# Turning tiles with the DMA engines instead of TensorE, on SyncE's queue, in a new instruction order

## The chip, the cores and the metric

The kernel runs on one core of one Trainium2 chip. The metric is the time on the device in microseconds (us). An execution has a state, fast or slow, given with each run: slow here means over 1.5% above the fastest run of the same kernel. Ratios below use fast runs alone, while the medians quoted are of all runs.

The engines: TensorE (PE for matmuls, PEld for loading weights), VectorE (DVE), ScalarE (ACT), GpSimd (POOL), SyncE (SP, which here does nothing but issue DMAs; "SPq" is its issue queue). Sixteen DMA engines move the data that all of them ask for.

## The reference

A gated delta rule over 4 batches of 8 heads, 768 tokens and 48 channels, followed by a mixing layer over tokens and channels:

```python
k_n = k / (np.linalg.norm(k, axis=-1, keepdims=True) + 1e-06)
for t in range(S):
    readout = np.einsum('bhd,bhde->bhe', q[:, :, t], state)
    y[:, :, t] = g[:, :, t] * readout
    v_old = np.einsum('bhde,bhd->bhe', state, kt)
    state = state + bt[:, :, :, None] * np.einsum('bhd,bhe->bhde', kt, vt - v_old)
# x: y with its heads side by side, (4, 768, 384)
theta = x @ w_theta
zr, zi = x * cos(theta), x * sin(theta)
u = x + einsum('ts,bsd->btd', w_tok_r, zr) + einsum('ts,bsd->btd', w_tok_i, zi)
return u + np.maximum(u @ w_ch, 0.0)
```

## The kernel before

The recurrence is worked in chunks of 128 tokens. There are 24 chunk tiles (4 batches of 6). For each, the kernel loads k, v and g, scales k, turns it (tokens to columns), forms two products of keys and queries, solves a triangular system, reads the state out, gates with g to get x, turns x, multiplies it by `w_theta`, takes sine and cosine, mixes over tokens with turned token weights, turns the mixed rows u and multiplies them by `w_ch`. Four kinds of tile are thus turned: keys (`kt`, 4 blocks of 128x128 each), x (`xT`, 3 blocks), mixed rows (`uT`, 3) and token weights (`wtokT`, 12 tiles of 6).

Every step is an operation with a name, its engine or a choice of engines ("ways"), and the pools that it takes a buffer from. A list `ORDER` holds the sequence of all 1,300 or so operations with the way of each; the instructions of each engine are issued in that order and each engine works through its own in order. So the place of an operation in `ORDER` is a schedule.

```python
SIZES = dict(
    k_raw=11, v_raw=6, g_raw=5, ktil=6, q_buf=2, qt=3, wtok=2, ksq=2, vs=5, kt=4, mt=4, at=4,
    x0=3, xa=3, xb=3, xT=3, sc=4, ut=3, uT=3, o=3, bank=8,
)
...
    def load(name, b, c):                      # k, v, g: all from SyncE
        def emit(way):
            src = {"k": k, "v": v, "g": g}[name]
            t = live[f"{name}{b}.{c}"] = sb(f"{name}_raw", [128, H, D], FP32)
            nc.sync.dma_start(t, src[b, :, c * C:(c + 1) * C, :].rearrange("h t d -> t h d"))
        add(f"{name}{b}.{c}", "SP", emit, (), ((f"{name}_raw", 0),))
...
        def emit_kt(way):                      # turn on TensorE, into PSUM
            t = live[f"ktp{n}"] = ps16(f"kt{n}")
            for p in range(NP):
                nc.tensor.transpose(
                    t[:, p, :], live[f"ktil{n}"][:, 2 * p:2 * p + 2, :].rearrange("p a d -> p (a d)"), ident
                )

        def emit_ke(way):                      # copy out of PSUM, on ACT or DVE
            live[f"kt{n}"] = sb("kt", [128, NP, C], BF16)
            evac(way)(live[f"kt{n}"], live.pop(f"ktp{n}")[:, 0:NP, :])
            done_with(f"kt{n}")
...
        def emit_out(way, x=""):               # stores: from SyncE too
            at0 = cols * halves.index(x)
            nc.sync.dma_start(out[b, tl * 128:(tl + 1) * 128, at0:at0 + cols], live[f"o{n}"][:, at0:at0 + cols])
```

x and u are turned in the same way (`xt` and `xe`, `utt` and `ue`), and the token weights too (`wt` and `we`).

Of the kernel before, what the change touches and what calls it, by code (L numbers as in the profile page):

```python
# [10 lines left out]
FP32 = mybir.dt.float32  # L11
# [4 lines left out]
ACT = mybir.ActivationFunctionType  # L16
# [9 lines left out]
TABLE_BATCHES = 3  # L26

# [5 lines left out]
    49, 2116, 3335, 0, 1, 4, 23, 24, 10, 52, 2, 3, 25, 26, 69, 70, 71, 7428, 22, 205, 29, 207, 72, 208, 209, 2259, 7,  # L33
    73, 1292, 2492, 446, 2075, 28, 5, 30, 31, 13, 411, 1277, 32, 273, 447, 413, 8, 448, 414, 415, 2465, 2286, 47, 43,
    41, 213, 44, 206, 2260, 419, 240, 67, 45, 46, 214, 450, 452, 219, 220, 50, 42, 2289, 2269, 451, 2270, 239, 2096,
    242, 2271, 244, 2272, 210, 225, 1275, 2294, 215, 33, 19, 245, 37, 275, 226, 2466, 216, 34, 243, 38, 276, 420, 412,
    425, 227, 228, 277, 2327, 426, 278, 2331, 16, 2083, 36, 217, 39, 40, 2300, 2301, 218, 2475, 2295, 2302, 2303, 248,
    61, 2328, 2329, 90, 2476, 2304, 2305, 88, 308, 2298, 2477, 58, 76, 2306, 2307, 2139, 249, 2126, 84, 79, 260, 86,
    11, 2391, 274, 2137, 185, 2478, 261, 85, 200, 77, 310, 2359, 2330, 87, 4358, 285, 229, 4359, 2479, 2480, 416, 312,
    2362, 287, 2469, 6, 230, 288, 2299, 345, 2481, 53, 2394, 264, 445, 2482, 347, 2397, 316, 289, 290, 453, 55, 2122,  # L40
    2506, 2507, 2399, 2339, 2340, 2341, 64, 2128, 14, 309, 81, 2470, 75, 82, 83, 2342, 460, 313, 2363, 2471, 461, 449,
    2502, 2510, 318, 2511, 456, 2343, 479, 481, 2344, 464, 457, 2368, 465, 186, 514, 2530, 516, 56, 480, 187, 2345,
    2346, 2514, 2515, 483, 2472, 485, 486, 2565, 487, 2332, 435, 484, 2537, 104, 2167, 4564, 518, 4565, 1274, 110,
    488, 322, 188, 231, 491, 2568, 549, 9, 378, 92, 265, 522, 98, 2541, 2542, 323, 2398, 232, 2543, 2544, 203, 2252,
    115, 317, 2569, 2372, 2237, 2373, 2538, 120, 2503, 380, 2429, 190, 2545, 2546, 266, 286, 299, 267, 2369, 2159,
    116, 326, 327, 95, 348, 1272, 2401, 2403, 2547, 2548, 12, 300, 470, 328, 329, 519, 524, 113, 301, 302, 330, 382,
    2432, 2549, 319, 2550, 2434, 2404, 331, 114, 173, 2380, 2381, 125, 492, 126, 201, 526, 17, 101, 344, 357, 1291,
    2400, 129, 2250, 131, 130, 358, 112, 2551, 2402, 359, 360, 132, 2552, 2165, 118, 127, 128, 551, 107, 2409, 2435,
    2169, 122, 193, 2242, 2410, 2411, 552, 123, 59, 124, 233, 191, 54, 334, 2240, 515, 2412, 365, 2576, 303, 1295,
    471, 234, 523, 2577, 366, 617, 619, 51, 436, 235, 4463, 2668, 4464, 685, 530, 531, 687, 2736, 437, 304, 472, 473,  # L50
    93, 1273, 621, 2486, 623, 305, 15, 335, 650, 180, 2580, 2581, 439, 440, 625, 626, 553, 618, 383, 624, 622, 2603,
    441, 2582, 369, 20, 527, 62, 2583, 627, 2427, 629, 268, 2436, 630, 307, 557, 2679, 269, 2680, 652, 653, 2440,
    2681, 2433, 536, 18, 2441, 336, 370, 390, 2682, 371, 175, 2604, 537, 372, 525, 60, 394, 337, 395, 237, 270, 505,
    689, 57, 691, 690, 2743, 692, 2745, 538, 539, 635, 338, 636, 2741, 396, 397, 540, 236, 339, 340, 183, 148, 558,
    373, 2232, 306, 272, 550, 398, 399, 506, 178, 637, 638, 474, 541, 563, 400, 401, 3117, 374, 2437, 176, 179, 271,
    391, 375, 2768, 507, 21, 162, 177, 342, 2556, 139, 376, 628, 1070, 564, 402, 509, 403, 341, 565, 475, 476, 1278,
    566, 2687, 2688, 404, 654, 510, 2615, 2453, 656, 722, 2616, 2742, 96, 651, 664, 181, 99, 1029, 658, 657, 659, 377,
    1071, 2559, 723, 665, 666, 2561, 182, 724, 163, 2774, 667, 569, 2632, 133, 2200, 406, 1030, 570, 668, 669, 136,
    154, 142, 155, 407, 408, 655, 2708, 151, 2560, 2619, 2620, 670, 671, 641, 586, 1031, 2635, 672, 158, 443, 1039,
    174, 477, 2710, 2776, 554, 94, 642, 159, 409, 588, 410, 1040, 673, 674, 156, 1032, 2638, 195, 153, 145, 2607, 160,  # L60
    1041, 686, 157, 643, 2744, 1072, 2640, 644, 675, 66, 97, 161, 3121, 542, 699, 543, 645, 2609, 169, 2709, 646,
    2608, 171, 755, 167, 170, 165, 1042, 1033, 647, 700, 166, 701, 172, 2711, 676, 1079, 164, 1034, 1080, 478, 702,
    1035, 1043, 2746, 573, 677, 574, 168, 1081, 648, 196, 197, 757, 703, 704, 678, 679, 1036, 1037, 1074, 823, 109,
    102, 721, 825, 826, 705, 706, 1075, 134, 824, 2806, 1082, 1083, 828, 2881, 2883, 589, 827, 1076, 2610, 856, 2642,
    2644, 1049, 829, 831, 137, 1077, 707, 858, 198, 708, 830, 2247, 1050, 140, 832, 837, 649, 709, 859, 1288, 63, 860,
    2910, 861, 711, 2775, 710, 100, 1051, 838, 712, 839, 840, 1293, 2882, 2914, 2916, 575, 576, 734, 65, 442, 1052,
    103, 841, 735, 842, 1084, 1085, 996, 105, 725, 2778, 585, 2911, 146, 2639, 598, 577, 843, 544, 2641, 599, 600,
    844, 2780, 2626, 2777, 736, 1285, 601, 1059, 1044, 2912, 135, 857, 737, 845, 1045, 602, 603, 2645, 1086, 579,
    1280, 738, 545, 891, 604, 546, 1087, 998, 680, 580, 1053, 2884, 1060, 847, 581, 739, 846, 870, 2643, 2913, 893,
    740, 605, 583, 606, 848, 999, 1054, 849, 871, 1061, 894, 1055, 741, 895, 607, 892, 897, 548, 742, 743, 1088, 1062,  # L70
    1056, 2947, 582, 1057, 713, 714, 850, 681, 547, 2730, 872, 873, 1063, 608, 1089, 609, 874, 896, 759, 1090, 901,
    875, 2809, 2811, 2951, 610, 744, 745, 611, 2948, 756, 1091, 876, 1000, 1139, 3050, 877, 143, 769, 2781, 2810, 108,
    2812, 612, 770, 878, 1004, 1078, 613, 790, 792, 879, 793, 2779, 771, 614, 1140, 772, 715, 2732, 716, 746, 747,
    927, 926, 615, 851, 852, 4950, 1058, 880, 881, 1290, 1046, 1047, 1294, 616, 1141, 905, 717, 2917, 906, 1048, 773,
    774, 1142, 4949, 1143, 760, 2813, 1001, 3054, 898, 2815, 907, 908, 962, 1064, 1008, 1092, 1093, 775, 909, 1099,
    1119, 1282, 1065, 2915, 3055, 882, 2816, 928, 1094, 1066, 776, 1120, 910, 911, 777, 929, 138, 1100, 1067, 883,
    778, 930, 2980, 149, 1038, 795, 3143, 912, 1281, 2982, 1009, 1101, 719, 913, 106, 1005, 2848, 914, 779, 780, 144,
    1121, 2814, 781, 2850, 791, 782, 915, 997, 916, 931, 2984, 794, 2844, 902, 1122, 1123, 1109, 940, 941, 1096, 2846,
    2731, 804, 2983, 783, 1097, 3051, 2851, 961, 748, 749, 2849, 963, 964, 938, 2847, 1102, 1124, 1103, 141, 1129,
    2981, 942, 750, 1125, 751, 2832, 805, 2845, 1126, 943, 806, 807, 785, 944, 752, 1130, 754, 1127, 1128, 786, 1279,  # L80
    1110, 945, 808, 809, 1104, 3153, 1144, 1098, 946, 947, 1111, 810, 811, 1112, 1113, 1145, 1146, 1147, 812, 1148,
    939, 813, 1131, 1169, 4883, 948, 949, 2952, 814, 815, 2985, 753, 4884, 966, 3019, 3021, 965, 967, 917, 968, 918,
    1189, 1132, 950, 951, 952, 718, 3020, 953, 969, 1199, 1190, 1170, 954, 955, 816, 1114, 1200, 1106, 1133, 817,
    3163, 884, 885, 1283, 4885, 818, 975, 819, 821, 1171, 976, 1107, 820, 1108, 886, 3022, 970, 977, 978, 147, 1149,
    1134, 1135, 1201, 979, 980, 822, 919, 1136, 1137, 1068, 1172, 1173, 981, 1150, 982, 1202, 1203, 1191, 1159, 983,
    984, 1204, 3253, 1179, 1151, 985, 986, 1206, 1192, 1207, 1010, 1011, 1152, 1153, 1116, 1208, 987, 887, 889, 1117,
    1012, 1118, 1180, 1013, 888, 956, 957, 958, 960, 1160, 1138, 4951, 890, 1181, 1174, 1182, 1014, 3223, 1176, 988,
    1161, 2968, 921, 1162, 959, 1193, 1194, 1177, 1015, 1183, 922, 2972, 989, 990, 2971, 1289, 3243, 1016, 1184, 1209,
    1252, 1017, 2973, 1196, 1197, 1018, 1154, 1155, 991, 992, 3041, 3042, 1210, 1019, 1020, 1253, 1185, 1156, 150,
# [49 lines left out]
def kernel(  # L139
# [76 lines left out]
    def setup():  # L216
# [14 lines left out]
        for t in q_bufs:  # L231
            nc.vector.memset(t[:, H * NCH * D:], 0.0)

    BANK = (("bank", 0),)
    EVAC = ("ACT", "DVE")

    def evac(way):
        return (nc.scalar.copy, nc.vector.tensor_copy)[way]

    def mul_on(way):  # L240
        return (nc.gpsimd, nc.vector)[way].tensor_mul
# [549 lines left out]
```

## Time and profile before

| | before |
|---|---|
| time, median of 4 runs | 185.31 us (183.7 to 186.19) |
| profiled run: span, granted clock | 186.1 us, 0.978 (slow, barely) |
| transposes of the four kinds on TensorE | 312 (128 columns each) |
| instructions on SyncE's queue | 98 DMAs, no transpose |
| SyncE's queue: issuing / not issuing | 108 / 78 us |

An issue occupies the queue for some time before the next can start; in the view by source line, the loads of k read (columns: count, then least/median/greatest ns of one issue, then first and last start):

```profile
L255 SPq DMA_DIRECT2D k_raw<-in_k_dram x24: 418/882/4580, 0.8 to 74.1; - x24
```

So a plain load takes at least 0.4 us of that queue, 0.9 in the median and up to 4.6 (that one at 28.5 us, while the DMA engines are full). The mean of all 72 loads is 1.3 us; in the probe e5 below, which moves less at a time, the median is 0.59. The last k tile is asked for at 74.1 us. From the waits of SyncE's queue (columns here and in all tables of waits: us in total, times, longest us):

```profile
SPq L720 <- DVE o L712: 62.3, 14, 9.2
```

### The profile page before, as it was taken

How to read it: one execution, taken by the hardware profiler on the slowest of the kernel's cores; microseconds unless marked ns; L12 is line 12 of the kernel's file. 1: busy time of each engine (PE TensorE's matmuls, PEld its weight loads, DVE VectorE, ACT ScalarE, POOL GpSimd, SP SyncE). 2: the span in 40 equal slices, each digit the busy share in tenths (PEclk: the TensorE clock that was granted, in tenths of full speed). 3: DMA queues.
4: the chain of work that ended last, by engine and by line, in shares of the span. 5: the costliest groups of instructions: out<-in, count | busy, mean ns of one | idle time of the engine just before them, and what ended most of it. 6: DMA issues, size and time to landing. Idle time of an engine off the chain costs nothing.

```text
span 186.1 us, 6390 instructions
## 1 busy us (share of the span) xinstructions
PE 169.4 (91%) x2578; PEld 121.6 (65%) x2579; DVE 150.6 (81%) x330; ACT 116.5 (63%) x240; POOL 125.5 (67%) x173
## 2 busy tenths in 40 slices
PE   2878889659899999999999999999999999999992
PEld 0256577456777777777777777676777766666651
DVE  5685999718799999999999998988898678871472
ACT  2665789914889998899895858756632520443130
POOL 3469378199896999999999899989581330713000
PEclk9999999956999999999999999999999999999998
DMA  5999979999997999999982061094021132503043
GB/s 116 186 202 179 181 142 173 169 200 149 207 223 153 199 213 178 205 156 205 221 168 46 26 153 46 0 211 95 0 88 42 31 101 83 132 0 127 4 168 129
DMA packets 85150, 24.70 MB, mean 133 GB/s; under 512 B 75488, under 2 KB 85088, under 8 KB 85120
## 3 DMA queue, kind: packets, MB, share of 16 engines
q1 hardware_dynamic: 78528, 18.98, 47.9%
q0 software_dynamic: 6592, 5.31, 19.2%
q8 instruction: 20, 0.33, 0.7%
q14 instruction: 10, 0.08, 0.1%
HBM read 24.87 MB, written 4.72 MB: 159 GB/s over the span
## 4 chain that ended last, share of the span: by engine, by line
PE 71%; DMA 10%; DVE 7%; POOL 4%; ACT 3%; issue 2%; SPq 1%; DVEq 0%; POOLq 0%
PE bank L667 23%; PE bank L515 8%; PE bank L704 6%; PE bank L615 5%; PE bank L431 5%; DMA k_raw<-in_k_dram 5%; DMA wtok<-in_moe_w_tok_i_dram 4%; PE bank L409 3%; PE bank L376 3%; PE bank L286 2%; PE bank L689 2%; PE bank L577 2%; PE bank L247 2%; PE bank L604 2%; PE bank L574 2%
## 5 line engine op out<-in xcount | busy, mean ns | idle before, releaser
L667 PE MATMUL bank<-z_all,wtokT 128*128 128x384 bf16 x288 | 58.1, 326 | 0.0
L515 PEld LDWEIGHTS <-mt 128*128 128x128 bf16 x768 | 30.8, 97 | 11.3 <-issue 4.6
L667 PEld LDWEIGHTS <-wtokT 128*128 128x128 bf16 x288 | 24.8, 97 | 12.2
L483 DVE TENSOR_TENSOR xa<-x,bank 128x384 bf16<-128x384 bf16 x45 | 24.5, 549 | 6.2 <-issue 3.7
L629 POOL TENSOR_TENSOR z_all<-x_sb,sc 128x384 bf16<-128x384 bf16 x22 | 20.2, 927 | 11.3 <-ACT sc L619 11.2
L515 PE MATMUL bank<-xa,mt 128*128 128x48 bf16 x576 | 25.5, 184 | 2.0 <-ACT xa L481 1.1
L636 POOL TENSOR_TENSOR z_all<-x_sb,sc 128x384 bf16<-128x384 bf16 x18 | 16.7, 930 | 10.9 <-ACT sc L623 10.4
L457 POOL TENSOR_SCALAR_AFFINE_SELECT at<-at 128x512 bf16<-128x512 bf16 x33 | 20.6, 634 | 4.1 <-ACT at L449 4.1
L404 POOL TENSOR_TENSOR vs<-v_raw,sqrtb 128x384 bf16<-128x384 f32 x23 | 19.0, 829 | 5.0 <-DMA v_raw<-in_v_dram 4.9
L449 ACT ACTIVATE at<-bank 128x512 bf16<-128x512 f32 x33 | 18.5, 602 | 6.2 <-PE bank L431 5.7
L400 POOL TENSOR_TENSOR ktil_ring<-k_raw,kscale 128x384 bf16<-128x384 f32 x19 | 16.4, 866 | 7.8 <-DVE kscale L357 6.5
L619 ACT ACTIVATE sc<-bank 128x384 bf16<-128x384 f32 x24 | 11.9, 497 | 13.9 <-DVE z_all L634 7.8
L449 ACT ACTIVATE mt<-bank 128x512 bf16<-128x512 f32 x27 | 15.9, 600 | 5.6 <-PE bank L431 4.8
L693 ACT COPY uT<-bank 128x384 bf16<-128x384 bf16 x17 | 8.3, 486 | 14.8 <-PE bank L689 7.6
L457 POOL TENSOR_SCALAR_AFFINE_SELECT mt<-mt 128x512 bf16<-128x512 bf16 x27 | 16.7, 633 | 0.1
L683 DVE TENSOR_TENSOR ut<-x_sb,bank 128x384 bf16<-128x384 bf16 x23 | 12.5, 549 | 4.9 <-PE bank L667 4.5
L712 DVE SCALAR_TENSOR_TENSOR o<-bank,ut 128x384 f32<-128x384 f32 (+1 forms) x25 | 13.2, 538 | 3.8 <-PE bank L704 2.1
L431 PEld LDWEIGHTS <-kt 48*128 48x128 bf16 x384 | 11.6, 97 | 6.5 <-ACT kt L415 2.5
L704 PE MATMUL bank<-w_ch_sb,uT 128*128 128x384 bf16 (+1 forms) x75 | 15.5, 320 | 0.2
L615 PE MATMUL bank<-w_theta_sb,xT 128*128 128x384 bf16 x72 | 15.6, 325 | 0.0
L451 DVE TENSOR_TENSOR mt<-bank,neg_mask 128x512 bf16<-128x512 f32 x21 | 13.9, 681 | 0.7 <-PE bank L431 0.7
L583 DVE TENSOR_TENSOR x_sb<-bank,g_raw 128x384 bf16<-128x384 f32 x24 | 13.2, 549 | 0.8 <-PE bank L577 0.7
(102 smaller groups left out, 380.6 us busy)
## 6 DMA issues: line engine op xcount, KB each, us to landing
k_raw<-in_k_dram SPq DMA_DIRECT2D x24, 192.0 KB, 4.1
v_raw<-in_v_dram SPq DMA_DIRECT2D x24, 192.0 KB, 6.7
g_raw<-in_g_dram SPq DMA_DIRECT2D x24, 192.0 KB, 4.4
out_dram<-o SPq DMA_DIRECT2D x23, 192.0 KB, 2.0
q_buf<-in_q_dram POOLq DMA_DIRECT2D x4, 576.0 KB, 7.8
wtok<-in_moe_w_tok_r_dram POOLq DMA_DIRECT2D x3, 384.0 KB, 6.9
wtok<-in_moe_w_tok_i_dram POOLq DMA_DIRECT2D x3, 384.0 KB, 7.3
w_theta_sb<-in_moe_w_theta_dram POOLq DMA_DIRECT2D x1, 288.0 KB, 5.8
```

Source lines behind the costliest of these rows:

```text
L400: mul_on(way)(ktil[:, :, 0:D], live.pop(f"k{n}"), _bcast_last(kscale[:, b, c], D))
L404: mul_on(way)(t.rearrange("p (h d) -> p h d", d=D), live.pop(f"v{n}"), _bcast_last(sqrtb[:, b, c], D))
L431: nc.tensor.matmul(t[j][:, p, :], kt[r, p, :], moving[r, p, :], start=True, stop=True)
L449: nc.scalar.mul(dst, gram_ps, -1.0)
L457: nc.gpsimd.affine_select(out=t, in_=t, compare_op=ALU.is_gt, fill=0.0, base=0, pattern=[[0, NP], [1, C]], channel_multiplier=-1,)
L483: nc.vector.tensor_add(t, live[x_name], p_x)
L515: nc.tensor.matmul(p_x[:, h * D:(h + 1) * D], head(live[f"mt{n}"], h), live[cur][:, h * D:(h + 1) * D], start=not way, stop=not way or h = ...
L615: nc.tensor.matmul(p_th, xT[:, cb, :], w_theta_sb[:, cb, :], start=(cb == 0), stop=(cb == NB - 1))
L629: (nc.vector if way == 3 else nc.gpsimd).tensor_mul(z_all[:, b % 3, c, 0], xt, live[f"si{n}"][:, 0])
L636: nc.gpsimd.tensor_mul(z[:, 1], xt, sc[:, 1])
L667: nc.tensor.matmul(p_mix, wtokT[:, i, s, tl * 128:(tl + 1) * 128], z_all[:, b % 3, s, 1 - i, :], start=(i, s) == parts[0] and not way, sto ...
L704: nc.tensor.matmul(p_ffn, uT[:, cb, :], w_ch_sb[:, cb, at0:at0 + cols], start=(cb == 0), stop=(cb == NB - 1))
```

## The change

The intent: TensorE is the busiest engine, so take transposes off it. A DMA from SBUF to SBUF that transposes on the way needs neither TensorE nor PSUM nor a copy out of PSUM. Each of the four kinds of tile gets a third way, chosen per tile in `ORDER`; all DMA transposes are on SyncE's queue. `ORDER` is new altogether: 69 tiles (22 of keys, 24 of x, 19 of mixed rows, 4 of token weights; 241 blocks) go by DMA.

```diff
-    EVAC = ("ACT", "DVE")
+    EVAC, BY_DMA = ("ACT", "DVE"), 2
+    TURN, TURNED = ("PE", "PE", ""), EVAC + ("SP",)
...
         def emit_kt(way):
+            if way == BY_DMA:
+                return
             t = live[f"ktp{n}"] = ps16(f"kt{n}")
...
         def emit_ke(way):
             live[f"kt{n}"] = sb("kt", [128, NP, C], BF16)
+            if way == BY_DMA:
+                nc.sync.dma_start_transpose(live[f"kt{n}"], live[f"ktil{n}"].rearrange("p h d -> p (h d)"))
+                return
             evac(way)(live[f"kt{n}"], live.pop(f"ktp{n}")[:, 0:NP, :])
...
-        add(f"ke{n}", EVAC, emit_ke, (f"kt{n}",), (("kt", 0),), ((f"kt{n}", "bank"),))
+        add(f"ke{n}", TURNED, emit_ke, (f"kt{n}",), (("kt", 0),), turned(f"kt{n}"), with_=f"kt{n}")
```

(cut: the same for x, u and token weights; the bias of the cosine given as a constant instead of a tile; the new list.)

## The prediction

> **What bounds the kernel now.** I read the page's busy line first, then the slices, then a table of stretches, then single groups and the DMA part.
>
> ```profile
> PE 169.4 (91%) x2578; PEld 121.6 (65%) x2579; DVE 150.6 (81%) x330; ACT 116.5 (63%) x240; POOL 125.5 (67%) x173
> PE   2878889659899999999999999999999999999992
> PEclk9999999956999999999999999999999999999998
> DMA  5999979999997999999982061094021132503043
> ```
>
> TensorE is busiest. Its slices split the run in two: up to slice 12 (some 60 us) it has holes, afterwards it is full to the end. The DMA engines are the mirror image: full to about 100 us, mostly idle later. The granted clock falls to 5 and 6 tenths in two slices, at 37 to 46 us. The table of stretches (PE, PEld, DVE, ACT, POOL busy; then clock, DMA share, GB/s) says the same in numbers:
>
> ```profile
> 30.00:40.00 10.00, 6.00 (x124) 4.48 (x119) 5.94 (x14) 6.89 (x16) 5.52 (x8) 0.89 0.99 181
> 40.00:50.00 10.00, 9.22 (x153) 7.37 (x150) 7.07 (x15) 6.04 (x13) 9.37 (x15) 0.77 1.10 174
> 60.00:80.00 20.00, 19.24 (x364) 15.05 (x364) 19.68 (x41) 18.80 (x43) 19.45 (x25) 1.00 1.04 197
> 120.00:140.00 20.00, 20.00 (x319) 14.49 (x316) 17.39 (x39) 10.08 (x21) 15.48 (x23) 1.00 0.39 92
> 160.00:180.00 20.00, 20.00 (x168) 12.98 (x167) 11.70 (x25) 6.43 (x14) 5.18 (x6) 1.00 0.20 71
> ```
>
> Busy PE can hide slack, since matmuls overlap. So I took the spacing of starts instead of the durations: in the timeline around 121 us three 128-column transposes start at 121.38 and the next group at 121.55, so 57 ns each; three 384-column matmuls follow each other in 0.49 us in the chain, so 163 ns each; 16 of the 48-column ones in 0.40 us, so 25 ns each. Multiplying the instruction counts of each stretch by such spacings gives, of TensorE time that is really needed: 34.8 us in the first 60, 18.1 in 60 to 80, 19.5, 19.3, 19.8, 20.1 and 20.3 in the five stretches of 20 us up to 180, and 155 us in all. From 80 us on TensorE has no slack: there, a microsecond taken off it is a microsecond of the end. In the first 60 us 25 us of it are unused, and what sets the pace there is other work: the chain of waits holds one wait of 8.7 us for a load of k at 28.5 to 37 us, and before it ACT, DVE and POOL steps.
>
> The transposes and the copies that bring them out of PSUM:
>
> ```profile
> L409 PE MATMUL bank<-ident,ktil_ring 128*128 128x128 bf16 x96 | 10.5, 241 | 3.1 <-POOL ktil_ring L400 3.1
> L689 PE MATMUL bank<-ident,ut 128*128 128x128 bf16 x72 | 7.8, 219 | 0.0
> L604 PE MATMUL bank<-ident,x_sb 128*128 128x128 bf16 x72 | 7.3, 219 | 0.0
> L608 ACT COPY xT<-bank 128x384 bf16<-128x384 bf16 x18 | 8.4, 485 | 6.0 <-PE bank L604 3.3 <-DVE mt L451 2.7
> L415 ACT COPY kt<-bank 128x512 bf16<-128x512 bf16 x14 | 8.2, 590 | 2.8 <-PE bank L409 2.8
> q1 hardware_dynamic: 78528, 18.98, 47.9%
> k_raw<-in_k_dram SPq DMA_DIRECT2D x24, 192.0 KB, 4.1
> out_dram<-o SPq DMA_DIRECT2D x23, 192.0 KB, 2.0
> ```
>
> See here that a transpose is counted as 219 to 241 ns busy though it costs 57 ns of the stream, and that loads land after 4.1 us while the DMA engines are full, stores (mostly later) after 2.0.
>
> **What the Trainium skill says.** "VectorE: DVE Perf Modes", section The three transpose paths, gives 390 ns for a 128x128 transpose on TensorE, ending in PSUM, and 1309 ns on the DMA crossbar, ending in SBUF. The trace shows 219 ns and a spacing of 57 for the first, so its figures are for one alone; it has no transpose by DMA. "DMA: Bandwidth & Descriptors", section Latency and other measured facts, gives transposes 261 GB/s, or some 350 to 400 in the contiguous case; no run shows that yet. The same page, Issuing engines are not separate DMA queues, says that DMAs of all issuers interleave on the same 16 engines: the trace agrees so far that loads of SyncE and of GpSimd share one full set of engines (share about 1.0, a median of 4.1 us to landing). Its section on two streams that transpose at once is met by putting all on one queue.
>
> **The change part by part.** By the order in which the changed program issues, 69 tiles turn by DMA: 22 of 24 of the keys (4 blocks of 128x128 each), all 24 of x (3 blocks), 19 of 24 of the mixed rows (3), 4 of 12 of the token weights (6). Removed from TensorE: 88 + 72 + 57 + 24 = 241 transposes, 241 x 57 ns = 13.7 us of stream. Of the blocks before, those after 60 us were 52 (keys), 63 (x), 72 (rows) and 36 (weights); of these I take 52 + 63 + 57 + 24 = 196 as gone, 11.2 us, all where TensorE is full.
>
> Added to TensorE: 22 identity additions in the solver and state read-out and one in the mix (41 + 12 + 2 against 26 + 5 + 1), 163 ns each, 3.7 us; about 17 of them come after the point that the old kernel reached at 60 us, so 2.8 us on the path. Warming matmuls go from 12 to 34, 22 x 213 ns = 4.7 us, all early, before TensorE is full: they fill holes and should cost nothing, and may spare the dip of the clock.
>
> PSUM copies vanish on both engines, and the new order shifts work. ACT: copies of keys, x, rows and weights 13 x 0.59 + 18 x 0.485 + 14 x 0.486 + 2 x 0.81 = 24.8 us less; evacuations after identity additions 22 x 0.485 = 10.7 more; 12 masks of 0.6 fewer, 7.2 less; small rest (3 squares, 2 states, one row, one table load of 1.3 fewer) 2.3 more: net 19 less, about 97. DVE: copies 8.7 less, 22 additions of 0.55 fewer, 12.1 less, 12 masks of 0.68 more, 8.2 more, rest 1 more: net about 11.5 less, about 139. POOL: 12 mask selections of 0.634 and some ten products of 0.82 to 0.93 fewer: about 16 less, 109. No engine gets worse; after 60 us none of these is at its limit, so this is worth slack and little time.
>
> Added to the DMA engines: 22 x 128 + 43 x 96 + 4 x 192 KiB = 7.9 MB. At the page's 261 to 400 GB/s an estimate of 20 to 30 us. Packets took 47.9 + 19.2% of 186, or 125 us, so the sum is 145 to 155 us of about 175: it fits, but tightly where the engines are full already. By the point of equal progress at 60 us some 17 transposes have been issued, an estimate of 5 to 7 us of DMA time in the phase that the loads pace.
>
> Sum: 11.2 - 2.8 = 8.4 us off the full phase. In the early phase I take off 2 more: the lost clock at 37 to 46 us and the relief of ACT and DVE (say 5) against the extra DMA time (say 3). 185.7 - 8.4 - 2 = 175.3, rounded 175.
>
> **The rivals.** First, latency takes the place of the removed work. A tile turned by DMA waits behind loads on a full set of rings, so 4 to 6 us instead of some 1.2 (four blocks and a copy). Only 4 key and 3 x buffers exist, and TensorE's order is fixed, so a late tile stalls everything behind it. For it: the DMA share of 1.0 up to 100 us, and a queue that issues in order, where a transpose waiting for its source holds back the loads behind it. Against: four independent batches, and loads that the new order spreads to later. This would give 180 to 188. Second, the DMA becomes the bound: if each block cost the page's 1309 ns with nothing overlapped, 241 blocks would be 315 us, and the kernel would take over 300. The bandwidth in the same skill speaks against it by a factor of ten, as does a choice made tile by tile, which leaves the first key tiles and the last rows on TensorE. A milder form, twice my DMA estimate, gives 185 to 200. Third, it goes better: the new order fills the 25 us that TensorE wasted in the first 60. With no DMA trouble, 165 to 170.
>
> **Range and chances.** Centre 175. The arithmetic of the full phase is firm to about 2 us; the early phase and the unknown cost of a transpose by DMA make the width: 166 to 185. Faster than 182 (over 2%): 0.77, since 8.4 us are 4.5% and must be half lost to miss it. Within 2%: 0.13, for the first rival. Slower: 0.10, for the second.
>
> **What would show it right or wrong.** Right: 71 transposes are left on TensorE of 312 (8 of keys, none of x, 15 of rows, 48 of weights), its matmul records fall by about 196 (241 less, 23 and 22 more), its slices are full from about 55 to 60 us to the end and end about 10 us sooner; the copies into kt and xT are nearly gone from ACT and DVE; a transpose by DMA lands in 2 to 6 us; no group of TensorE has idle of more than 2 us put down to a DMA into kt, xT or uT. Wrong: TensorE waits for such a DMA in the table of waits; the issue queue spends long in transposes that wait, and loads behind them land late; the DMA share is 9 to the end; the clock dips in more slices than before; or transposes land after 8 us and more.

## The result, and the profile after

The changed kernel is correct and slower: 219.42 us median of 4 runs (218.11 to 221.88) against 185.31. The ratio is 1.183 (95% interval 1.171 to 1.195). Ratios are computed as the mean time of one kernel's fast runs over the mean of the other's fast runs of the same rounds, so not quite the ratio of the medians quoted. The profiled run of the changed kernel (span 220.1 us, clock 0.922) counts as slow, but the clocks of its fast runs were no better (0.906 to 0.933), and its time is in the middle of theirs.

The page after: busy time of the engines, then the 40 slices of TensorE, of its granted clock and of the DMA engines, the hardware DMA queue (packets, MB, share of the 16 engines), and the shares of the chain that ended last:

```profile
PE 173.9 (79%) x2383; PEld 115.6 (53%) x2383; DVE 144.9 (66%) x298; ACT 98.4 (45%) x210; POOL 110.7 (50%) x151
PE   1293888877985698457999989885988899799993
PEclk9999555999998599955999999999999999999999
DMA  6999999999999869699998997656875963153335
q1 hardware_dynamic: 111584, 26.88, 69.6%
PE 38%; DMA 25%; DVE 13%; SPq 6%; issue 6%; POOL 5%; ACT 5%; DVEq 0%; POOLq 0%; ACTq 0%
```

The removed work is gone as planned: 195 matmul records fewer, ACT at 98.4 us and POOL at 110.7. But TensorE no longer has a full phase. Before, its slices were full from the 12th or so to the end; now they have holes to the end, and the chain that ended last lies on PE for 38% (71% before) and on DMA for 25% (10%). The clock falls to 5 in six slices (to 5 and 6 in two before). One line of the table of stretches shows the loss (columns as in the prediction):

```profile
60.00:80.00 20.00, 14.71 (x244) 10.43 (x241) 17.26 (x32) 12.01 (x27) 10.66 (x15) 0.83 1.04 165
```

The stretch from 60 to 80 us, where before had TensorE busy 19.24 us with DVE and POOL above 19 too, now has no engine above 17.3: everybody waits for somebody. For whom, the table of waits says (cut; its longest entry is 43.0 us of ACT for TensorE's products of x, which in turn wait for the tiles of x below):

```profile
POOL vs L416 <- DMA v_raw<-in_v_dram: 24.5, 7, 9.5
DVE x_sb L600 <- DMA g_raw<-in_g_dram: 12.1, 7, 2.7
PE bank L637 <- DMA xT<-x_sb: 9.5, 5, 4.1
PE bank L448 <- DMA kt<-ktil_ring: 5.5, 5, 2.9
```

Read this from the bottom. TensorE waits for turned tiles, 15 us in these two lines; but more is lost to plain loads: GpSimd waits 24.5 us for v (4.9 us before) and VectorE 12.1 for g, and neither load has changed. They are late. Yet a load of v or g or a transpose, once issued, is not slow (columns: KB where given, and median us from issue to landing):

```profile
v_raw<-in_v_dram SPq DMA_DIRECT2D x24, 192.0 KB, 3.9
...
xT<-x_sb SPq DMA_TRANSPOSE x24, 3.6
```

v landed after 6.7 us before and after 3.9 now, faster, and g after 4.4 and 4.0. (k, all of it in the first 100 us, is slower: 4.1 and 6.0.) So v and g are issued late. The view by source line of the new transposes and of the loads:

```profile
L628 SPq DMA_TRANSPOSE xT<-x_sb x24: 1178/1232/4406, 47.9 to 198.3; - x24
L260 SPq DMA_DIRECT2D k_raw<-in_k_dram x24: 433/812/4664, 0.8 to 96.3; - x24
L260 SPq DMA_DIRECT2D v_raw<-in_v_dram x24: 438/580/3595, 3.9 to 169.0; - x24
```

A transpose holds SyncE's queue for at least 1.18 us. The last load of k starts at 96.3 us instead of 74.1, the last of v at 169.0 instead of 121.1. In the timeline of SyncE (start us, duration us) there are stretches without a gap, in which v and g stand between transposes:

```profile
118.13 1.21 SPq L628 DMA_TRANSPOSE xT<-x_sb  x1
119.39 0.58 SPq L260 DMA_DIRECT2D g_raw<-in_g_dram  x1
120.02 2.86 SPq L718 DMA_TRANSPOSE uT<-ut  x2
122.92 0.58 SPq L260 DMA_DIRECT2D v_raw<-in_v_dram  x1
123.60 6.13 SPq L298 DMA_TRANSPOSE wtokT<-wtok  x2
```

The sum of the durations of all SyncE's DMA issues gives 185 us of issuing (69 transposes 103 us, the rest 82) and 36 without, in 220 (108 and 78 before). A queue that had room is now nearly full. That gives the theory to test:

**Theory Q (queue).** The loss is in SyncE's one in-order issue queue: a DMA transpose takes about 1.2 us of it against 0.6 for a plain DMA, and a transpose that has to wait for its source holds up the loads behind it. **Rivals:** the DMA engines' traffic (small packets); the round trip of a turned tile as such; the new order itself, above all its slow start. A further rival, the lower granted clock, had no experiment of its own. The runs speak against it as the main cause: e12 loses 16 us at a clock of 0.973 to 0.989, and e13 took 205.8 us at 0.924 and 205.9 at 0.958.

### The profile page after: what moved, and what is told of

It reads as the page before. It is cut to its first block, busy times and chain, and to the rows that moved or that the text cites. A ratio compares the mean times of both kernels' runs of the same rounds, so it can differ in the third digit from the quotient of the medians.

```text
span 220.1 us, 5959 instructions
## 1 busy us (share of the span) xinstructions
PE 173.9 (79%) x2383; PEld 115.6 (53%) x2383; DVE 144.9 (66%) x298; ACT 98.4 (45%) x210; POOL 110.7 (50%) x151
## 3 DMA queue, kind: packets, MB, share of 16 engines
q1 hardware_dynamic: 111584, 26.88, 69.6%
## 4 chain that ended last, share of the span: by engine, by line
PE 38%; DMA 25%; DVE 13%; SPq 6%; issue 6%; POOL 5%; ACT 5%; DVEq 0%; POOLq 0%; ACTq 0%
PE bank L689 12%; DMA xT<-x_sb 8%; DMA g_raw<-in_g_dram 5%; DMA k_raw<-in_k_dram 4%; PE bank L448 4%; PE bank L532 4%; PE bank L637 4%; DMA uT<-ut 4%; DMA kt<-ktil_ring 4%; PE bank L731 3%; SPq L260 3%; PE bank L494 2%; SPq L718 2%; PE bank L388 2%; POOL z_all L651 2%
## 5 line engine op out<-in xcount | busy, mean ns | idle before, releaser
L416 POOL TENSOR_TENSOR vs<-v_raw,sqrtb 128x384 bf16<-128x384 f32 x21 | 17.3, 829 | 24.5 <-DMA v_raw<-in_v_dram 24.5
L637 PE MATMUL bank<-w_theta_sb,xT 128*128 128x384 bf16 x72 | 16.6, 342 | 11.2 <-DMA xT<-x_sb 9.5
L500 DVE TENSOR_TENSOR xa<-x,bank 128x384 bf16<-128x384 bf16 x37 | 19.9, 548 | 7.8 <-PE bank L532 6.5
L651 POOL TENSOR_TENSOR z_all<-x_sb,sc 128x384 bf16<-128x384 bf16 x19 | 17.5, 928 | 12.2 <-ACT sc L641 12.2
L346 DVE TENSOR_REDUCE nsq<-ksq 128x8 f32<-128x384 f32 x24 | 12.7, 545 | 16.4 <-POOL ksq L341 9.1
L600 DVE TENSOR_TENSOR x_sb<-bank,g_raw 128x384 bf16<-128x384 f32 x24 | 13.2, 552 | 13.7 <-DMA g_raw<-in_g_dram 12.1
L498 ACT CAST xa<-bank 128x384 bf16<-128x384 f32 x30 | 14.1, 484 | 17.6 <-PE bank L532 16.9
L466 ACT ACTIVATE at<-bank 128x512 bf16<-128x512 f32 x27 | 15.7, 600 | 9.0 <-PE bank L448 8.7
L468 DVE TENSOR_TENSOR mt<-bank,neg_mask 128x512 bf16<-128x512 f32 x27 | 17.9, 684 | 2.2 <-PE bank L448 2.1
L658 POOL TENSOR_TENSOR z_all<-x_sb,sc 128x384 bf16<-128x384 bf16 x17 | 15.8, 929 | 5.8 <-ACT sc L645 5.8
L474 POOL TENSOR_SCALAR_AFFINE_SELECT at<-at 128x512 bf16<-128x512 bf16 x27 | 17.5, 657 | 1.4 <-ACT at L466 1.3
L468 DVE TENSOR_TENSOR at<-bank,neg_mask 128x512 bf16<-128x512 f32 x21 | 14.3, 683 | 4.8 <-PE bank L448 2.5
L474 POOL TENSOR_SCALAR_AFFINE_SELECT mt<-mt 128x512 bf16<-128x512 bf16 x21 | 13.1, 636 | 8.0 <-ACT mt L466 8.0
```

The lines of the kernel that those rows point to most:

```text
L416: mul_on(way)(t.rearrange("p (h d) -> p h d", d=D), live.pop(f"v{n}"), _bcast_last(sqrtb[:, b, c], D))
L466: nc.scalar.mul(dst, gram_ps, -1.0)
L468: nc.vector.tensor_mul(dst, gram_ps, _bcast_mid(neg_mask, NP))
L474: nc.gpsimd.affine_select(out=t, in_=t, compare_op=ALU.is_gt, fill=0.0, base=0, pattern=[[0, NP], [1, C]], channel_multiplier=-1,)
L500: nc.vector.tensor_add(t, live[x_name], p_x)
L637: nc.tensor.matmul(p_th, xT[:, cb, :], w_theta_sb[:, cb, :], start=(cb == 0), stop=(cb == NB - 1))
```

## The experiments

Eighteen kernels ran. "Queue" in this table is the sum of SyncE's issue times in the profiled run, and "gaps" the rest of that run's span; the ratio is that to before's fast runs of the same rounds. For e14 the interval (1.017 to 1.031) reaches below 2%; those of e1 to e4 start at 1.061 or above. The profiled runs of before, of the changed kernel, of e2, e12 and e14 counted as slow.

| run | what | result | median us | ratio | queue / gaps, us |
|---|---|---|---|---|---|
| before | | correct | 185.31 | | 108 / 78 |
| changed | | correct | 219.42 | 1.183 | 185 / 36 |
| e1 | new order, no DMA transposes | correct | 231.2 | 1.257 | 89 / 140 |
| e2 | old order, the 69 tiles by DMA | correct | 266.7 | 1.444 | 158 / 109 |
| e3 | plain copy for each transpose | wrong | 195.66 | 1.068 | 136 / 57 |
| e4 | v and g on ACT's queue | correct | 225.32 | 1.231 | 136 / 88 |
| e6 | two half copies for each transpose | wrong | 214.89 | 1.172 | 171 / 41 |
| e7 | copy in 256-byte packets | wrong | 195.7 | 1.063 | 148 / 47 |
| e8 | old start, then new order | wrong by a slip | 217.75 | 1.189 | 186 / 30 |
| e10, e11, e12 | old order up to a point; 15, 34, 53 tiles | correct | 185.19, 200.98, 200.02 | 1.004, 1.089, 1.084 | 130 / 54, 149 / 50, 171 / 30 |
| e13 | old order, 23 tiles with slack | correct | 207.28 | 1.121 | 128 / 77 |
| e14 | the same 23, issued late | correct | 188.6 | 1.024 | 131 / 58 |
| e15 | e13, loads earlier | correct | 194.45 | 1.057 | 125 / 69 |
| e16 | changed kernel, loads earlier | correct | 235.05 | 1.274 | 188 / 45 |
| e17 | e14, loads earlier | correct | 193.3 | 1.053 | 133 / 57 |
| e18 | e14 less 5 key tiles | correct | 186.12 | 1.002 | 121 / 63 |
| e19 | e14 less 2 key tiles | correct | 186.05 | 1.004 | 126 / 58 |

### First attempts: order and transposes apart (e1, e2)

e1 keeps the new order and puts all 69 tiles back on TensorE with a copy; e2 keeps the old order and sends the same 69 by DMA.

```diff
# e1, in the new ORDER, for each of the 69 tiles
-  ke (way 2: SyncE)
+  kt (TensorE), ..., ke (way 0 or 1: ACT or DVE), where a PSUM bank is free
# e2, in the old ORDER, for each of the same 69 tiles
-  kt (TensorE), ke (ACT or DVE)
+  ke (way 2: SyncE) at the place of ke
```

> The new order, with all 69 tiles turned on TensorE and copied out by ACT or DVE again; nothing is turned by DMA. Theory A (the DMA transposes cost the time, by the issue queue of SyncE that takes 1.2 us for each and holds the loads behind them, or by the DMA engines): 182 to 195 us, near the kernel before, with the bytes of its queue back at 19 MB. Theory B (the new order is the slow part: more identity additions, more warming, loads later): 205 us and more, close to the 219 of the change.

> The old order, with the same 69 tiles turned by DMA at the places where their PSUM copies stood. Theory A: slower than before by 10% or more, 205 to 240 us, since the queue meets the same 69 issues of 1.2 us and its order was not even made for them. Theory B: within 5% of the kernel before, 178 to 194 us.

Both came out slower than the changed kernel: 231.2 and 266.7 us. So e1 lies in theory B's range (205 us and more), though above the 219 that B pointed to, and e2 above theory A's. I take neither as settled. In e1 I placed 138 operations by rule into an order made without them, and the in-order engines then stall on each other (ACT waits 26.9 us for TensorE before copies of u, GpSimd 24.4 for ACT's sine), so its time need not be the price of the order. e3, below, bounds that price: the same order with plain copies runs at 195.66 us (with the transposes off TensorE). In e2 SyncE's queue stands idle for 85 us ahead of transposes and GpSimd waits 44.4 us for v, a case of what the series from e13 on takes apart. An order and its ways belong together; swapping one alone measures the mismatch.

### What a transpose costs over a plain copy (e3, e6, e7)

These keep the changed kernel, its order and its 69 DMAs from SBUF to SBUF, and only alter the kind of DMA. The results are wrong, as nothing is turned; the instructions that follow are the same.

```diff
# e3: a plain copy of the same bytes
-                nc.sync.dma_start_transpose(live[f"xe{n}"], xt)
+                nc.sync.dma_start(live[f"xe{n}"].rearrange("p a b -> p (a b)"), xt)
# e6: the same in two halves, so two issues
+                for a in range(2):
+                    nc.sync.dma_start(live[f"xe{n}"].rearrange("p a b -> p (a b)")[:, a * 192:(a + 1) * 192], xt[:, a * 192:(a + 1) * 192])
# e7: one issue, but in packets of 256 bytes as the transpose has
-            live[f"xe{n}"] = sb("xT", [128, NB, 128], BF16)
+            live[f"xe{n}"] = sb("xT", [128, NB, 144], BF16)[:, :, 0:128]
+                nc.sync.dma_start(live[f"xe{n}"], xt.rearrange("p (a b) -> p a b", b=128))
```

> The changed kernel with each DMA transpose replaced by a plain DMA copy of the same bytes between the same two tiles (result wrong on purpose): same order, same waits, same queue, but an issue should take some 0.57 us instead of 1.2 and the packets are of 768 and 1024 bytes. If the cost of the transpose itself (its issue and its small packets) makes the loss: 175 to 195 us. If it is the waits in the queue (a transfer that waits for its source holds the loads behind it) or the round trip that every tile makes: 205 us and more.

> The run with plain copies, with each copy made by two DMAs of half the width (result wrong on purpose): some 1.15 us of the issue queue for a tile, as a transpose takes, and the same bytes in packets of 384 and 512 bytes. If the longer issue is what a transpose costs over a copy: 208 to 222 us, near the changed kernel. If the crossbar and its small packets are: 193 to 203 us.

> The run with plain copies into padded tiles (result wrong on purpose), so that every packet is of 256 bytes, as many packets as the transposes make, with one issue of about 0.6 us for a tile. If the number of small packets on the DMA engines is what a transpose costs over a copy: 205 us and more. If the issue is: 193 to 201 us.

e3 runs at 195.66 us, so some 21 of the 34 us lost belong to the transpose as against a copy (1.183 less 1.068; by the medians, of different rounds, 24). It could be the packets or the queue. The hardware queue's line of e7 (packets, MB, share):

```profile
q1 hardware_dynamic: 110480, 26.88, 66.6%
```

e7 moves nearly as many packets as the changed kernel (111,584) and takes nearly as much of the DMA engines (66.6% of its span, 130 us, against 69.6%, 153 us), and is as fast as e3: 195.7 us. e6 takes less of the engines (100,448 packets, 57.6%, 122 us) and costs 214.9 us. What e6 shares with the changed kernel is the queue: 171 us of issue, against 136 and 148 in the two fast ones. And with the full queue the late loads come back. Waits in e6:

```profile
POOL vs L417 <- DMA v_raw<-in_v_dram: 18.0, 7, 11.7
DVE x_sb L602 <- DMA g_raw<-in_g_dram: 9.1, 5, 3.2
```

In e3 the second isn't in the table, and the first is

```profile
POOL vs L416 <- DMA v_raw<-in_v_dram: 7.8, 5, 2.7
```

So as many small packets cost nothing in e7, and what takes the time in e6 is issuing on the queue; 23 us more of queue (e7 to e6) cost 19 us of time. (For the 153 us of the changed kernel, more than e7's 130, at most the 2 to 5 us are left that lie between e6 and it.) The time isn't in proportion over the whole range, though: e3 to e7 added 12 us of queue at no cost. (e6 also signals twice as often; the gaps in its queue are 41 us against e3's 57, so it doesn't wait more for that.) A later landing of the turned tile, a rival that had no run, can be read from the same traces: from issue to landing the tiles of x, of keys and of u took 3.6, 3.4 and 2.7 us in the changed kernel and 3.0, 4.0 and 2.0 in e3 (medians), so it accounts for little.

### The disputed cost by itself (e5)

A kernel that does nothing but move data: rows of twelve loads, twelve transposes of 128x384, loads and transposes in turn, twelve plain copies, then other widths, then four transposes in a chain, each group after the one before has landed. Its output is wrong, which doesn't matter for the time.

```diff
+        for i in range(N): turn(i, 384)                # tr[i] <- src
+        for i in range(N): load(i); turn(i, 384)
+        for i in range(N): copy(i, 384)
+        for i in range(1, 5): turn(i, 384, tr[i - 1])  # each needs the one before
```

> A kernel that only moves data (result wrong on purpose), in groups of 12 that wait for each other: loads of 192 KB; transposes of 128x384; both alternating; plain copies of 128x384; loads and copies alternating; transposes of 128x512 and of 128x128; then five dependent transposes. If the issue queue is what a transpose costs, its issues follow each other at 1.2 us and 12 take some 15 us, with the engines less than half busy. If the DMA engines are, the alternating group takes about the sum of the two alone (some 13 + 6 us and more) and the loads in it slow down. The dependent ones show the round trip: 2.3 to 2.6 us each.

From the timeline of SyncE:

```profile
24.02 15.57 SPq L39 DMA_TRANSPOSE tr<-src  x12
46.33 1.20 SPq L39 DMA_TRANSPOSE tr<-src  x1
47.58 0.57 SPq L36 DMA_DIRECT2D ld<-in_k_dram  x1
...
75.11 7.62 SPq L42 DMA_DIRECT2D tr<-src  x12
157.28 8.24 SPq L39 DMA_TRANSPOSE tr<-tr  x4
```

Twelve transposes take 15.57 us of the queue, 1.3 us each with the gap between issues; twelve plain copies of the same size 7.62, or 0.64. A transpose and a load in turn take 1.9 us a pair. The width hardly counts: the mean issue was 1.22, 1.25 and 1.26 us at 128, 384 and 512 columns. While the twelve were issued, their packets took only 5.8 us of the DMA engines' 15.6 (my sum over the packets), so the issue, not the crossbar, sets the rate. In the chain a transpose takes 2.35 us from issue to the next one's (8.24 us is four issues and the three waits between them). The sum for the changed kernel: 69 x (1.25 - 0.57) = 47 us more of queue than plain copies would take; its queue had 49 more than e3's.

### Loads on another queue (e4)

```diff
-            nc.sync.dma_start(t, src[b, :, c * C:(c + 1) * C, :].rearrange("h t d -> t h d"))
+            (nc.sync if name == "k" else nc.scalar).dma_start(t, src[b, :, c * C:(c + 1) * C, :].rearrange("h t d -> t h d"))
```

> The changed kernel with the 48 loads of v and g issued by ACT's queue; transposes, loads of k and stores stay on SyncE's. The DMA engines move the same bytes. If the one issue queue is the bound (it spends 189 of 220 us in issues): SyncE is relieved of some 40 us and the time falls to 185 to 205 us, though ACT pays 48 issues of 0.6 us. If the DMA engines are the bound: 212 to 225 us, no gain.

225.32 us, a miss for the queue, at the edge of what was expected if the DMA engines were the bound (212 to 225; e7 is what speaks against that). SyncE's queue fell to 136 us of issue as intended, yet GpSimd's waits for v grew from 24.5 us to 32.2. Now the loads stand in ACT's own stream, which is in order as well and waits for PSUM results; I take it that they are late for that reason, which was not tested. The run doesn't support the theory; if that reading is right, it doesn't refute it either, as it moved the head of the line to another engine.

### Is it the start? (e8, e10, e11, e12)

e8 takes the first 145 steps from the old order and the rest from the new; e10, e11 and e12 the first 1,080, 740 and 430, so that 15, 34 and 53 tiles go by DMA.

```diff
# e8, e10, e11, e12
-ORDER = [new list]
+ORDER = [first 145 / 1080 / 740 / 430 of the old list] + [what is left, in the new list's order]
```

> The changed kernel with the first 145 steps in the old order (the four key tiles in them on TensorE), then the new one; 65 tiles still turn by DMA. All three runs with the new order reach 10 us of needed TensorE work at 42 to 45 us, the old kernel at 31. If the new start is a loss of its own: 202 to 210 us. If the start was late only because of the DMA transposes or is made up later: 214 to 221 us.

> The first 1080 steps in the old order (useful work up to 90 of 126 us), the rest in the new one: 15 tiles turn by DMA, all when few loads are left. Issue-queue theory: 15 x 1.25 us fit in an idle queue, so 181 to 187 us. If a DMA transpose costs by itself as in the whole change (34 us over 69, 0.5 us each): 190 to 194 us.

> The same with the first 740 steps in the old order: 34 tiles turn by DMA. Issue-queue theory: from about 101 us on the queue has 34 x 1.25 and some 40 other issues of 0.57 us, 65 us for the 80 that are left, so a little late at times: 184 to 195 us. Proportional to the number of tiles: 200 to 204 us.

> The same with the first 430 steps in the old order (66 us of the old kernel): 53 tiles turn by DMA. Issue-queue theory: 53 x 1.25 and some 60 issues of 0.57 us, 100 us and the waits for room on the rings, against 120 us left: 198 to 212 us. Proportional: 208 to 214 us. If the loss of the change sits in its first stage: 185 to 190 us.

e8 gives a wrong result by a slip of mine (the ways of some pairs of matmul and evacuation were mixed at the seam); its instruction counts are nearly the same, so I read its time with that reserve: 217.75 us, no better than the changed kernel. To compare progress I counted needed TensorE work (without transposes, warming and identity additions; 126 us in all, in units of the spacings of the prediction) along the traces: before has done 10 us of it at 35 us, the changed kernel at 52 and e8 at 48, and 60 us of it at 110, 138 and 133. So a start that is some 4 us faster did not shorten the run (1.189 against 1.183 for the changed kernel). That the end doesn't wait for the start is suggested by this, from a run with a wrong result, and not shown.

e10 costs nothing (185.19 us, 1.004), so 15 late tiles are free and bring nothing. e11 and e12 cost 16 us each though the number of tiles differs by 19. e11 (200.98 us) missed the queue theory's 184 to 195 us and lies in the range for a loss in proportion to the tiles (200 to 204); e12 (200.02) lies in the queue theory's. In the progress count e11 loses 11 us at the seam of the two orders and about keeps the pace after it; e12 loses 8 there and 7 more by the end. Their queues differ: e11's stands idle 28 us ahead of transposes with 149 us of issue, e12's 12 us with 171. The loss comes in hiccups more than by the tile. That led to the next series.

### Waiting at the head of the queue (e13 to e17)

e13 keeps the old order and sends 23 tiles (74 blocks) by DMA which had 5 us or more of slack in the trace of before, after 85 us. Each transpose stands right behind its source in the order.

```diff
# e13, for each of 23 tiles in the old ORDER
-  kt (TensorE), ke (ACT or DVE)
+  ke (way 2: SyncE), directly behind the step that writes its source
```

> The old order, with 23 tiles turned by DMA: only those whose source is ready after 85 us (when the DMA engines empty and TensorE is full) and whose first reader comes 5 us or more later in the trace of the kernel before, each issued right after its source. 74 blocks off TensorE, 74 x 57 ns = 4.2 us. If the issue queue and late tiles are what the change lost by, this has neither: 180 to 183 us. If DMA transposes are costly wherever they stand: 187 us and more.

207.28 us, 22 more than before and far from expected, with a queue that issued for 128 us of 204. Here "the queue is full" does not explain the loss. The longest wait of SyncE's queue, and then of GpSimd:

```profile
SPq L720 <- DVE ut L707: 14.9, 4, 7.0
```

```profile
POOL vs L418 <- DMA v_raw<-in_v_dram: 21.6, 5, 7.0
```

One such case in the timelines of SyncE, of GpSimd and of TensorE (in square brackets: idle before it, and what ended that):

```profile
96.16 1.82 SPq L262 DMA_DIRECT2D g_raw<-in_g_dram  x2
103.80 1.80 SPq L630 DMA_TRANSPOSE xT<-x_sb  x1
105.65 0.58 SPq L262 DMA_DIRECT2D v_raw<-in_v_dram  x1
```

```profile
108.84 0.83 POOL L418 TENSOR_TENSOR vs<-v_raw,sqrtb 128x384 bf16<-128x384 f32 x1 [6.21 <-DMA v_raw<-in_v_dram]
```

```profile
110.90 0.22 PE L534 MATMUL bank<-x,mt 128*128 128x48 bf16 x1 [4.07 <-POOL mt L476]
```

SyncE stands still from 97.98 to 103.80 us, because the next in line is a transpose whose x isn't ready. The load of v behind it needs nothing, but starts at 105.65. GpSimd, in order, waits 6.21 us for v, its mask for the next chunk comes after that, and TensorE waits for the mask. A tile that could wait has stopped one that could not. By the progress count the run loses its time in stretches (from about 83 to 120 us and near 140), and outside them it is about as fast as before.

If that is the cause, it can be taken away without removing a transpose: issue it later, when its source has long been there (e14), or put the loads ahead of it (e15), or both (e17); e16 puts the loads ahead in the changed kernel.

```diff
# e14: the same 23 tiles
-  ke (SyncE), directly behind its source
+  ke (SyncE), as late as leaves 4 us of TensorE work before its first reader
# e15: e13, and for each load of v and g
-  load at its place
+  load 40 places earlier in ORDER, within its buffers
# e17: e14 with e15's loads;  e16: the changed kernel, loads of k, v, g 60 places earlier
```

> The same 23 tiles of the old order as in the run with slack, but each DMA transpose stands in program order not right behind its source but as late as it may, about 4 us of TensorE work ahead of its first reader, so that the source has long been done when SyncE comes to it. Head-of-line theory (a transpose that waits for its source holds up the loads behind it): the waits of SyncE for transposes' sources (about 29 us in that run) fall to under 5 us, the waits of POOL for v fall from 21.6 to under 8 us, and the time from 207 to 181-187 us. Rival (each transpose costs what it costs in queue time and traffic, wherever it stands): 203-210 us.

> The run with slack unchanged but for the loads of v and g, each 40 places earlier in program order, so that they stand ahead of the transposes that waited. Head-of-line theory: SyncE still waits for the sources, but what is behind it has been loaded: POOL's waits for v fall from 21.6 to under 8 us, the time from 207 to 184-192 us (less than the other run, as stores and k loads still stand behind). Rival (cost where it stands): 203-210 us.

> Both of the first two runs' edits at once (transposes late, loads early). Head-of-line theory: 178-185 us, the best of the three; a rate at or below before's 184-186 would be a version that uses the DMA transposes without loss. Rival: 203-210 us.

> The changed kernel itself with nothing altered but the loads of v, g and k, 60 places earlier in program order each (within their buffers). If the loss is mainly that loads stand behind waiting transposes (head of line): 195-208 us. If the queue is simply full (189 us of issue in 220), moving loads ahead makes the transposes later by as much and the time stays at 214-222 us.

e14 takes 188.6 us: of the 22 us that the 23 tiles cost, all but 4 are gone, with the same transposes on the same queue. SyncE's idle time ahead of transposes (a sum over the trace) fell from 56.7 us to 8.6 while its issue time stayed (128 and 131 us), and in the timeline the same stretch now reads

```profile
97.26 0.79 SPq L262 DMA_DIRECT2D v_raw<-in_v_dram  x1
98.14 1.51 SPq L630 DMA_TRANSPOSE xT<-x_sb  x1
99.75 0.53 SPq L262 DMA_DIRECT2D v_raw<-in_v_dram  x1
```

GpSimd's waits for v are 9.8 us instead of 21.6:

```profile
POOL vs L418 <- DMA v_raw<-in_v_dram: 9.8, 6, 4.9
```

e15, by the other way, gives 194.45 us and waits for v of 3.7 us; the transposes still wait in it (the queue is idle 42.9 us ahead of them) but hold up less. Both were just outside their ranges and far from the rival's 203 to 210, so the wait at the head of the queue is the main cost in the old order. e17 was expected to be the best and is not (193.3): with v and g moved up at the start as well, the first loads of k come later (ACT's wait for k is 9.5 us instead of 3.5), and the run is 5 us behind e14 after the first 5 us of TensorE work. That cost lies in e15 too; moving loads up is not free where the engines are full.

e16 got worse, 235.05 us. TensorE's matmuls on keys waited 5.5 us for turned tiles in the changed kernel and wait 16.3 us now: in a queue with 188 us of issue, what is put ahead pushes something else back. It met neither range (195 to 208, 214 to 222), and it isn't a clean test, since some 10 us of its loss come before the first 10 us of TensorE work are done, from the same late start as in e17. It does agree with the changed kernel's own sums: its queue is idle only 15.9 us ahead of transposes. There the sum of issue times is what holds the loads, more than waiting.

### The rest of e14 (e18, e19)

One stall is left in e14, at 125 us: TensorE waits for a key tile and then for x, in the queue behind three stores that, with the waits between them, took from 112.86 to 119.86. e18 gives TensorE all five key tiles back, e19 only the two at that place.

```diff
# from e14
-  ke2.5, ke3.3 by DMA            (e18: ke2.4, ke3.5, ke3.4 too)
+  kt on TensorE, ke on ACT or DVE, as in before
```

> The run with the tiles issued late, less its five key tiles, which go back to TensorE; 18 tiles (54 blocks) stay with the DMA engines. In the late run one stall is left, at about 125 us, where TensorE waits for a key tile and then for a load of g, both behind stores that wait on SyncE. If that stall is all that separates it from before, this one goes to 181-184 us (54 x 57 ns = 3.1 us of TensorE work less than before's 184.3). If what is left is spread cost, 186-188 us.

> The run with the tiles issued late, less only the two key tiles that stand in the stall at about 125 us; 21 tiles stay. Head of line: 180-184 us, a little below the other run if the three other key tiles do no harm. Spread cost: 186-188.5 us.

186.12 us (1.002, interval 0.995 to 1.010) and 186.05 us (1.004, interval 0.998 to 1.010): the stall was those two tiles, and without them the kernel is level with before. But level is all. The 21 tiles of e19 take 66 transposes, 3.8 us, off TensorE, and the expected 180 to 184 us did not come; both runs lie in the ranges that were set for the rival, a cost spread over the tiles (186 to 188, 186 to 188.5). In its profiled run, at full clock, TensorE is busy 165.2 us, 4.2 less than in before's profile (which was a slow run at 0.978, so part of this is the clock), and four of its slices after the 12th are at 7 or 8 tenths where before has 9 throughout: some of the freed time shows as holes. What opens them is not settled. No version that I ran beats before.

## Why the prediction was wrong

- **What bounds the kernel, and what is removed:** right. 71 transposes were left, the matmul records fell by 195 (predicted about 196), ACT came to 98.4 us (97), DVE to 144.9 (139), POOL to 110.7 (109).
- **"Added to the DMA engines: ... it fits":** this is the step that failed. It priced the transposes in bytes against the bandwidth of 16 engines and nowhere in the time of the one queue that issues them. That term was missing: 69 transposes held SyncE's queue for 103 us (1.5 us each in the kernel; 1.25 alone in e5), which brought it from 108 to 185 us of issue. The DMA engines' own term was too small as well: the share of the hardware queue went from 47.9% of 186 to 69.6% of 220, 64 us more where 20 to 30 were predicted. But e7, whose packets take 40 us more than before's, is no slower than e3.
- **"Sum: 11.2 - 2.8 = 8.4 us off the full phase":** the premise, a TensorE without slack, was read from before and did not hold for the changed kernel. It lost its full phase, because v, g and the turned tiles come late; then a microsecond taken off TensorE is worth nothing. Even in the old order the premise was too strong: e10 (with the new order's tail) and e19 took 45 and 66 transposes (2.6 and 3.8 us) off TensorE in its full phase, and were not faster (1.004 each, with intervals from 0.998).
- **"In the early phase I take off 2 more":** it went the other way, some 18 us lost by the first 10 us of work, but e8 suggests that the end hardly waits for this. The warming matmuls did not spare the dip of the clock: six slices at 5 tenths instead of two at 5 and 6.
- **The first rival** had the direction and the mechanism ("a queue that issues in order, where a transpose waiting for its source holds back the loads behind it"), and e13 and e14 show just that. Its size, 180 to 188, was too small: head of line alone cost 19 us with only 23 tiles (1.121 to 1.024 by changing places alone), and 69 tiles fill the queue besides. What was named against it, "loads that the new order spreads to later", did not help: those loads stood among transposes on the same queue.
- **The second rival** (1309 ns a block, nothing overlapped) was rightly doubted: the cost is per instruction of up to 512 columns, not per block. I then took the bandwidth to be all that was left.
- **What would show it wrong:** of the five signs three came (TensorE waiting for turned tiles, loads behind transposes late, more dips of the clock). Two did not, and did not matter: transposes landed after 2.7 to 3.9 us (medians of the four kinds; the slowest single one 8.9), and the DMA engines were not full to the end.

Of the 34 us lost, by the ratios: some 21 are the transpose as against a plain copy, by e3, and 19 of these come back with a second issue for each tile, by e6. The other 13 (e3 against before), and the further gain of 10 that even e3 did not show, are not divided: the round trip of a tile through SBUF, waiting at the head of the queue and the new order are all in them, and e1, which was to tell the order's part, failed to.

## What to carry to other kernels

Price each DMA on the queue that issues it, in time per issue, before pricing its bytes: sum the issue times of a queue in the profile, and see whether the additions fit. On a queue in order, place an issue where its source is sure to be ready, and never ahead of loads that an engine will need first; a late place for 23 transposes was worth 19 us. And if moving work off the busiest engine leaves it waiting, the work removed is worth nothing: look at who feeds it first.

## What the Trainium skill lacked or had wrong

- "DMA: Bandwidth & Descriptors", section Issuing engines are not separate DMA queues, calls the sequencer's time to initiate a DMA "usually small relative to the DMA itself". Here it was not small: 185 of 220 us of SyncE's queue, 0.57 us for a plain DMA and 1.25 for a transpose. The page's section DMA Transpose (X-bar) gives no issue time (another section of the page, on a later chip, has sequencer cycles of earlier generations, but none for tiles of this size inside SBUF), and the page says nothing on waiting for a source at the head of an issuing queue (19 us in e13 against e14).
- "Advanced Engine Details and Errata", section X-Bar Transpose (TRN2), says that transposes by DMA are as fast as regular ones. In e5, twelve of 128x384 took 15.57 us of the queue and twelve plain copies of the same size 7.62.
- "VectorE: DVE Perf Modes", section The three transpose paths, gives 1309 ns for a 128x128 transpose on the DMA crossbar without saying of what. In e5 a transpose took 1.22 us of issue at 128 columns and 1.26 at 512, so it is nearer a cost per instruction; in a chain of four they followed each other after 2.35 us.
